# Gate's third and fourth row blocks by seven products instead of eight, and ten early transform steps moved two stages later

## The chip, the cores and the metric

One of the eight cores of a Trainium2 chip runs the kernel. The metric is device microseconds of one execution; the number to predict is the median of three runs. Two names are used throughout: PE is TensorE, the matrix engine, which multiplies a stationary 128x128 block by up to 512 moving columns and adds into a bank of PSUM; DVE (VectorE) and ACT (ScalarE) prepare its operands and take its results out of the banks. POOL (GpSimd) and SP (SyncE) here mostly issue DMAs. Each engine works through its own list of instructions in the order in which they were written.

## What is computed

Two branches over the same input x (2 x 4096 x 640) are mixed by a sigmoid gate:

```python
g = sigmoid((x * gate_w).sum(-1))
a = A(x)      # rfft2 over the 4096 tokens, block-diagonal complex MLP with 4 blocks, soft shrink, irfft2
b = (gelu(x @ w_gate) * (x @ w_up)) @ w_down      # 640 -> 1728 -> 640
out = g * a + (1 - g) * b
```

The change touches the two products `x @ w_gate` and `x @ w_up`, and the first step of the transform in A.

## The kernel before

**The arithmetic.** Everything is fp32 accuracy from fp32r products: an operand is split into a high part (ACT copies it, `high`, L276) and a low part (DVE subtracts the copy, `low`, L279), and a product is three matmuls (high x high, high x low, low x high, `prod`, L472).

**The stages.** First (0 to 1350 us of the span) the products with w_gate and w_up run in three groups of weight tiles: tiles 0 to 3, 4 to 7 and 8 to 13. In each group, all 16 token pairs (512 tokens each, split in two halves of 256) pass by; one token pair with one group is a key, and `keys` (L1311) lists the 48 of them. Then comes the transform with its MLP (to about 1810 us), then the inverse transform with w_down (to the end).

**A quad.** `quad` (L503) does one weight tile (128 gate and 128 up columns) for one token pair. The 640 rows of the weight are five blocks of 128. Blocks 0 and 1 of gate and all of up already go by a seven-product scheme over (gate, up) x (two token halves); blocks 2 and 3 of gate against the first token half are one ordinary product, `g2` by `b21`, of six matmuls into a bank of its own, added on DVE to the partial sum p1:

```python
X = half(); run(X, prod(w["g1"], x_of(o, "b11", ("k4", 0))))
p1 = T("p1"); copy(p1, X)                                        # ACT, L509
C = half(); run(C, prod(w["s3"], x_of(o, "t3", ("k4", 1))))
A = half(); run(A, prod(w["g2"], x_of(o, "b21")))                # six matmuls
nc.vector.tensor_add(p1, A, p1)                                  # L525
run(X, prod(w["s2"], x_of(o, "t2", "t5")), first=False)          # goes on in the bank of p1
```

A quad has 54 matmuls of 256 columns. Bank X is used again and again within it: ACT copies an intermediate sum out (p1, u2, u4), and PE then adds the next product on top. So PE may only go on in a bank when the copy, or the DVE addition, that reads it is over. Three pieces of a quad (`half5`, `half3`, `half4`, L537 to L549) run inside the next quad. Results go to DRAM (`hD`) by a store of 128x4x128 per quad.

**The order around it.** The kernel writes its own schedule. Each quad has seven hooks; `slots` says which small step is issued at which hook of which key. Among them: splitting the next key's tokens (`x_prep`, L426; raw tiles loaded by SP, the sums t1 to t4 formed on DVE, L441), preparing the next group's weights (`w_prep`, L313, eight steps for each weight tile, mostly on DVE), and the first transform steps (`a_split`, `a_gate`, `a_step`, L621 to L634), 64 of them with four matmuls each of 320 columns, placed by `steps_a` (L1382) and `A_POINTS`. The next group's first `w_prep` begins in the last but one key of a group (place 14, hook 10), the others in the last key and the first two of the next group.

**Buffers.** Tiles come from pools of fixed slots: `big` 18, `mid` 14, `small` 18, `tiny` 15, and eight PSUM banks. An instruction that first writes a new tile waits until the last reader of the slot's former tile is done, whichever engine that is, and everything behind it on its own engine waits with it.

Of the kernel before, what the change touches and what calls it, by code (L numbers as in the profile page):

```python
# [15 lines left out]
P = 128  # L16
# [9 lines left out]
NPAIR = 13  # L26

# [186 lines left out]
def spectral_mix_kernel(ctx: ExitStack, tc: tile.TileContext, a):  # L214
# [50 lines left out]
    wdl = dram.tile([P, 7 * 320], F32, name="wdl")  # L265

# [37 lines left out]
    WG, XT, XO, RAW = {}, {}, {}, {}  # L304

# [7 lines left out]
    def w_prep(t, plain=False):  # L313
# [17 lines left out]
        def st0():  # L331
            if not plain:
                gate_high()
            if t < NPAIR:
# [76 lines left out]

    made = lambda key: key[0] == 0 or key == (1, 0)

    def x_raw(key, names=("b11", "b21", "b12", "b22", "k4")):
        d = XT.setdefault(key, {})
        for n in names:
            if key[0] != 1 or made(key) or n != "b12":
                r = d[n] = small([P, 512], name="xraw")
                ld(r, a["xT"][key[1], ("b11", "b21", "b12", "b22", "k4").index(n)])
# [6 lines left out]
    def x_prep(key, k, eng=nc.vector):  # L426
# [43 lines left out]
        return [src, hi, lo]  # L470
# [32 lines left out]
    def quad(key, t, hook):  # L503
# [8 lines left out]

        X = half()
        run(X, prod(w["g1"], x_of(o, "b11", ("k4", 0))))
        p1 = T("p1")
        copy(p1, X)
        hook(0)
# [3 lines left out]
        run(C, prod(w["s3"], x_of(o, "t3", ("k4", 1))))  # L521
        hook(2)
# [5 lines left out]
        u2 = T("u2")  # L528
        copy(u2, X)
        hook(4)  # L530
        old[1]()
        hook(5)
        old[2]()
        hook(6)
        v = {}

        def half5():  # L537
# [3 lines left out]
            gelu(p1, p1)  # L541
            nc.vector.tensor_add(u4, C, u4)  # L542

        def half3():
            run(X, prod(w["s4"], x_of(o, "b22")), first=False)
            h = v["h"] = small([P, 512], name="h")
            gelu(h[:, 256:], X)

        def half4():  # L549
            run(C, prod(w["u2"], x_of(o, "t4")), first=False)  # L550
            nc.vector.tensor_add(u2, C, u2)  # L551
            h = v["h"]
            nc.vector.tensor_mul(h[:, 256:], h[:, 256:], v["u4"])
            nc.vector.tensor_mul(h[:, :256], u2, p1)  # L554
            h_store(key[1], t, h)
        Q.append([half5, half3, half4])

# [753 lines left out]
    keys = [(gr, tp) for gr in range(3) for tp in ([1, 2, 3, 4, 0, *range(5, 16)] if gr == 1 else range(16))]  # L1311
# [59 lines left out]
    A_POINTS = {0: ((1, 3, 4, 5, 8),), 1: ((1, 3, 4, 5, 8), (12, 14, 16, 21, 23)), 2: ((0, 2, 3, 4, 9), (24, 25, 27, 28, 29))}  # L1371
# [10 lines left out]
    steps_a = [(i, j) for i in (*range(2, 12), *range(17, 30), *range(32, 46)) for j in range(1 if i < 16 else 2)]  # L1382
# [18 lines left out]
    for k in range(4):  # L1401
        spread(*((0, 11), (0, 20), (1, 2), (1, 10))[k], w0[k][4 if k else 1:])
    for k, (l, pb) in enumerate(((1, 0), (1, 1), (2, 0), (2, 1))):
# [5 lines left out]
    for gr in range(2):  # L1409
        for k, t in enumerate(groups[gr + 1]):  # L1410
            (i, j), (i2, s) = [((13, 3), (14, 10)), ((14, 3), (15, 8)), ((15, 0), (15, 17)), ((15, 2), (16, 4)), ((15, 3), (16, 12)), ((15, 1), (15, 25))][k]
# [179 lines left out]
```

## Time and profile before

| what | us |
|---|---|
| median of three runs | 2537.26 (2536.99 to 2538.45) |
| the profiled execution, its own time | 2535.42 |
| its span in the trace | 2533.7 |
| PE busy | 2527.2 |
| DVE busy | 2052.9 |
| ACT busy | 1492.7 |

The profiled execution lies 1.84 us under the median, and 1.72 us of its own time are outside the span. PE is busy for all but some 6 us, and the granted clock is full throughout. "Busy" of PE joins overlapping records, so it hides gaps shorter than the overlap; how long a matmul really takes is read from the chain of waits, where a run of matmuls stands with its count and its time.

### The profile page before, as it was taken

To read this page: it belongs to the slowest core of one execution; us is meant where nothing else is said; L and a number is where in the kernel's file an instruction comes from. 1 tells how busy PE (TensorE), PEld (TensorE's weight loads), DVE (VectorE), ACT (ScalarE), POOL (GpSimd) and SP (SyncE) were. 2 spreads that over 40 slices of the span, in tenths; PEclk is the share of its full clock that TensorE was granted. 3 is DMA by queue.
4 is the path that set the end of the run, shared out by engine and by line. 5 is a ranking of instruction groups with operands and counts; after the bars stand their busy time and mean duration, and the time that the engine had idled before them with its cause. 6 is when DMAs were issued, how large, how long until landed. Compare 5 with 4: busy or idle time off the path is not lost.

```text
span 2533.7 us, 54552 instructions
## 1 busy us (share of the span) xinstructions
PE 2527.2 (100%) x20299; PEld 2522.9 (100%) x20299; DVE 2052.9 (81%) x4218; ACT 1492.7 (59%) x3494; POOL 372.4 (15%) x379
## 2 busy tenths in 40 slices
PE   9999999999999999999999999999999999999999
PEld 9999999999999999999999999999999999999999
DVE  7878767777777767766667788888999999899998
ACT  6655555666665655655556788787644444444443
POOL 0000000000000000000003111111133333333332
PEclk9999999999999999999999999999999999999999
DMA  6566647676767677766767354548744444344432
GB/s 231 195 214 197 212 169 234 203 240 210 223 204 253 192 227 226 232 219 209 225 224 229 121 166 141 169 144 263 288 146 150 156 157 139 134 151 157 154 130 103
DMA packets 345982, 483.77 MB, mean 191 GB/s; under 512 B 24748, under 2 KB 221996, under 8 KB 345716
## 3 DMA queue, kind: packets, MB, share of 16 engines
q1 hardware_dynamic: 330884, 438.47, 54.2%
q0 software_dynamic: 14832, 41.82, 4.6%
q8 instruction: 160, 2.62, 0.4%
q14 instruction: 106, 0.87, 0.1%
HBM read 300.55 MB, written 179.64 MB: 190 GB/s over the span
## 4 chain that ended last, share of the span: by engine, by line
PE 96%; DVE 2%; DMA 1%; ACT 1%; issue 0%; SPq 0%; DVEq 0%; ACTq 0%
PE bank L483 54%; PE bank L1234 22%; PE bank L295 14%; PE bank L811 3%; PE bank L645 1%; PE bank L892 1%; PE bank L893 1%; DMA wraw<-in_wgu_dram 0%; DVE w L279 0%; DVE xo L279 0%; PE bank L894 0%; DVE xd L441 0%; DMA xraw<-in_xT_dram 0%; DVE uu L1239 0%; DVE h L554 0%
## 5 line engine op out<-in xcount | busy, mean ns | idle before, releaser
L483 PE MATMUL bank<-xo,w 128*128 128x256 f32 x11676 | 1351.0, 277 | 0.7 <-ACT u L509 0.6
L483 PEld LDWEIGHTS bank<-xo,w 128*128 128x128 f32 x11676 | 1342.2, 188 | 1.7 <-ACT u L509 1.3
L1234 PE MATMUL bank<-wx,ho 128*128 128x320 f32 x3844 | 560.6, 306 | 0.0
L1234 PEld LDWEIGHTS bank<-wx,ho 128*128 128x128 f32 x3844 | 557.1, 188 | 0.0
L509 ACT ACTIVATE u<-bank 128x256 f32<-128x256 f32 x408 | 156.6, 384 | 253.4 <-PE bank L483 248.3
L279 DVE TENSOR_TENSOR ho<-hraw,ho 128x640 fp32r<-128x640 f32 (+3 forms) x384 | 273.8, 754 | 21.4 <-ACT ho L276 18.4
L276 ACT ACTIVATE ho<-hraw 128x640 fp32r<-128x640 f32 x320 | 166.8, 571 | 91.5 <-PE bank L1234 66.0
L509 ACT ACTIVATE p<-bank 128x256 f32<-128x256 f32 x204 | 78.6, 385 | 148.4 <-PE bank L483 61.9
L279 DVE TENSOR_TENSOR xo<-xraw,xo 128x512 fp32r<-128x512 f32 x209 | 143.2, 686 | 23.9 <-ACT xo L276 23.2
L542 DVE TENSOR_TENSOR u<-bank,u 128x256 f32<-128x256 f32 x204 | 85.9, 421 | 89.2 <-ACT u L509 86.6
L279 DVE TENSOR_TENSOR xs<-xr,xs 64x640 fp32r<-64x640 f32 x128 | 104.9, 820 | 58.1 <-ACT xs L276 55.6
L295 PE MATMUL bank<-wm,h 128*128 128x320 f32 (+1 forms) x792 | 137.7, 309 | 0.0
L276 ACT ACTIVATE xo<-xraw 128x512 fp32r<-128x512 f32 x209 | 131.0, 627 | 6.1 <-DMA xraw<-in_xT_dram 4.3
L551 DVE TENSOR_TENSOR u<-bank,u 128x256 f32<-128x256 f32 x204 | 85.5, 419 | 60.0 <-PE bank L483 59.3
L647 DVE TENSOR_TENSOR as<-bank,as 64x320 f32<-64x320 f32 x256 | 113.7, 483 | 24.9 <-ACT as L646 23.7
L295 PEld LDWEIGHTS bank<-wm,h 128*128 128x128 f32 (+1 forms) x792 | 117.9, 185 | 1.4
L598 POOL MEMSET h<- 64x512 f32 x16 | 8.4, 522 | 749.8 <-PE bank L645 437.5
L483 PE MATMUL bank<-wx,ho 128*128 128x320 f32 x764 | 116.3, 307 | 0.0
L525 DVE TENSOR_TENSOR p<-bank,p 128x256 f32<-128x256 f32 x204 | 86.6, 424 | 36.5 <-PE bank L483 31.9
L483 PEld LDWEIGHTS bank<-wx,ho 128*128 128x128 f32 x764 | 112.1, 188 | 0.0
L276 ACT ACTIVATE ho<-hs 128x640 fp32r<-128x640 f32 (+1 forms) x128 | 69.0, 570 | 70.2 <-DVE ho L279 51.1
L646 ACT ACTIVATE as<-bank 64x320 f32<-64x320 f32 x256 | 96.8, 427 | 16.4 <-PE bank L645 13.9
(168 smaller groups left out, 3669.6 us busy)
## 6 DMA issues: line engine op xcount, KB each, us to landing
xo<-xD SPq DMA_DIRECT2D x124, 512.0 KB
xraw<-in_xT_dram SPq DMA_DIRECT2D x225, 256.0 KB
hD<-h SPq DMA_DIRECT2D x224, 256.0 KB
hraw<-hD SPq DMA_DIRECT2D x128, 320.0 KB
xD<-xo POOLq DMA_DIRECT2D x64, 512.0 KB, 4.3
sc<-scr SPq DMA_DIRECT2D x65, 320.0 KB
xr<-in_x_dram SPq DMA_DIRECT2D x64, 320.0 KB
scr<-as SPq DMA_DIRECT2D x64, 320.0 KB
```

Source lines behind the costliest of these rows:

```text
L276: nc.scalar.activation(dst, src, AF.Copy, scale=scale)
L279: eng.tensor_sub(dst, src, hi.bitcast(F32))
L295: nc.tensor.matmul(dst, l, r, start=i == 0, stop=i == len(ops) - 1)
L483: nc.tensor.matmul(dst, l, r, start=first and i == 0, stop=i == len(ops) - 1, skip_group_check=True)
L509: copy = lambda d, s_: nc.scalar.activation(d, s_, AF.Copy)
L525: nc.vector.tensor_add(p1, A, p1)
L542: nc.vector.tensor_add(u4, C, u4)
L551: nc.vector.tensor_add(u2, C, u2)
L646: nc.scalar.activation(stg[hi, cs], pa[lo, :320], AF.Copy)
L647: nc.vector.tensor_add(stg[hi, cs], pa[hi, :320], stg[hi, cs])
L811: nc.tensor.matmul(pz[:, kp * P:(kp + 1) * P], SC[b, c, kp][:, o:o + P], ft, start=True, stop=True)
L1234: nc.tensor.matmul((X, Y)[k], *op, start=n[k] == 0 and not (more and k), stop=n[k] == tot[k] - 1, skip_group_check=True)
```

## The change

For token pairs 3 to 14 of groups 0 and 1 (`deep`), the product of gate's blocks 2 and 3 leaves the quads. Two weight tiles (t, t+1) x two row blocks form a 2x2 matrix of weight blocks, two row blocks x the first halves of two token pairs (tp, tp+1, tp odd) a 2x2 matrix of token blocks, and their product is made by seven block products of three matmuls each (`deep_parts`) instead of eight. The seven run one at a time between the pieces of the two quads that follow, in two banks, and each is added on DVE to one of four waiting partial sums:

```diff
+    def deep(key):
+        return key[0] < 2 and FIRST <= key[1] < 15
...
+        def go(m, n, first, dst):
+            if n not in b:
+                b[n] = bank()
+            acc = b[n][:, :256]
+            for i, (l, r) in enumerate(prod([wa[m]], [xa[m]])):
+                nc.tensor.matmul(acc, l, r, start=first and i == 0, stop=i == 2, skip_group_check=True)
+            nc.vector.tensor_add(dst, acc, dst)
+        def f0():
+            go("m2", 0, True, p11)
+        def f1():
+            go("m1", 1, True, p11)
+            g11()
...
+        E.extend([(0, f0), (1, f1), (2, f2), (3, f3), (0, f4), (1, f5), (3, f6), (0, f7)])
```

In such a quad the ordinary product is skipped, and gelu and the last multiplication (`end`) wait until the seven products are in:

```diff
-        A = half()
-        run(A, prod(w["g2"], x_of(o, "b21")))
-        nc.vector.tensor_add(p1, A, p1)
+        if not dp:
+            A = half()
+            run(A, prod(w["g2"], x_of(o, "b21")))
+            nc.vector.tensor_add(p1, A, p1)
```

The weight sums for it are made by `w_deep` (four small DVE operations, then a split), the token sums by `x_deep` (two DVE operations of 256 columns at each of two places, five splits, two of them of 512 and three of 256 columns). Group 0 stores the split token sums to a new DRAM tensor `xA` through POOL (`mid` tiles of 128x1024 and `small` tiles of 128x512), group 1 loads them back through SP and no longer loads and splits `b21`. Half of the result stores become two of 128x2x128.

The schedule changes with it: no transform step is left in group 0, and ten keys of group 2 have three instead of two; group 1 begins with token pairs 1, 2, 0; the first weight tile of the next group is prepared from the start of a group's last key on, not from the key ahead:

```diff
-    keys = [... ([1, 2, 3, 4, 0, *range(5, 16)] if gr == 1 else range(16))]
+    keys = [... ([1, 2, 0, *range(3, 16)] if gr == 1 else range(16))]
-    steps_a = [(i, j) for i in (*range(2, 12), *range(17, 30), *range(32, 46)) for j in range(1 if i < 16 else 2)]
+    steps_a = [(i, j) for i in (*range(17, 30), *range(32, 46)) for j in ((0, 1) if i < 32 else (0, 1, 2) if 32 < i < 43 else (0, 2))]
-            (i, j), (i2, s) = [((13, 3), (14, 10)), ((14, 3), (15, 8)), ...
+            (i, j), (i2, s) = [((14, 1), (15, 0)), ((14, 3), (15, 8)), ...
```

The order on the engines, first on PE inside a deep stretch of group 0. Before, a quad of token pair 4 and a transform step in it (w_152 to w_156 are blocks of weights; rows of one line stand together with their count):

```order
L483 MATMUL bank<-xo,w_152 128x256 x9
L483 MATMUL bank<-xo,w_418 128x256 x9
L483 MATMUL bank<-xo,w_358 128x256 x9
L483 MATMUL bank<-xo,w_152 128x256 x6
L483 MATMUL bank<-xo,w_358 128x256 x9
L483 MATMUL bank<-xo,w_780 128x256 x3
L483 MATMUL bank<-xo,w_781 128x256 x3
L645 MATMUL bank<-xs,f_828 128x320 x2
L483 MATMUL bank<-xo,w_418 128x256 x6
```

Now, a quad with four of the seven products (L693) in it:

```order
L562 MATMUL bank<-xo,w_298 128x256 x9
L693 MATMUL bank<-xo,w_158 128x256 x3
L562 MATMUL bank<-xo,w_286 128x256 x9
L562 MATMUL bank<-xo,w_654 128x256 x9
L693 MATMUL bank<-xo,w_158 128x256 x3
L562 MATMUL bank<-xo,w_654 128x256 x9
L693 MATMUL bank<-xs,w_1014 128x256 x3
L562 MATMUL bank<-xo,w_540 128x256 x3
L562 MATMUL bank<-xo,w_541 128x256 x3
L562 MATMUL bank<-xo,w_286 128x256 x6
L693 MATMUL bank<-xo,w_1014 128x256 x3
```

The six matmuls in the middle are gone, products of three stand between the others, and the transform step's matmuls (L645) are no longer in this group.

Second, DVE at the end of group 0, where the next group's first weight tile begins to be prepared (in brackets what an instruction waits for; wt are weight sums, p1, u2, u4, h and pb partial sums, xo split tokens). Before:

```order
L542 TENSOR_TENSOR u4_5388<-bank_5317,u4_5388 128x256 [waits Activation_49]
L525 TENSOR_TENSOR p1_5376<-bank_5404,p1_5376 128x256 [waits PE_49]
L339 TENSOR_TENSOR wt_5414<-wraw_5285 128x256 [waits DMAHW0_49]
L340 TENSOR_TENSOR wt_5416<-wt_5414,wraw_5283 128x256 [waits DMAHW7_49,DVE_49]
L279 TENSOR_TENSOR xo_5402<-xraw_5281,xo_5402 128x512 [waits DMAHW6_49,DMASW2_49,Activation_49]
L441 TENSOR_TENSOR xd_5420<-xraw_5279,xraw_5277 128x512 [waits DMAHW5_49,DMAHW4_49,DMAHW1_49]
L345 TENSOR_TENSOR wt_5416<-wraw_5283,wraw_5285 128x256
```

Now:

```order
L346 TENSOR_TENSOR wt_5406<-wraw_5187 128x256 [waits DMAHW2_49,DVE_49]
L347 TENSOR_TENSOR wt_5408<-wt_5406,wraw_5185 128x256 [waits DMASW2_49,DMAHW1_49,DVE_49,PE_49]
L640 TENSOR_TENSOR u4_5422<-bank_5315,u4_5422 128x256 [waits DMAHW0_49,Activation_49]
L352 TENSOR_TENSOR wt_5408<-wraw_5185,wraw_5187 128x256
L353 TENSOR_TENSOR wt_5406<-wraw_5185,wt_5408 128x256 [waits DVE_49]
L281 TENSOR_TENSOR xo_5411<-xd_5355,xo_5411 128x512 [waits DMASW6_49]
L694 TENSOR_TENSOR pb_4880<-bank_5439,pb_4880 128x256
L281 TENSOR_TENSOR w0_5404<-wraw_5185,w0_5404 128x5x128
L616 TENSOR_TENSOR p1_5396<-bank_5446,p1_5396 128x256
L365 TENSOR_TENSOR wt_5407<-wraw_5187,wraw_5185 128x128
L366 TENSOR_SCALAR wt_5407<-wraw_5187 128x128
L694 TENSOR_TENSOR p1_5296<-bank_5399,p1_5296 128x256
```

The second weight sum (wt, L340 before, L347 now) waited for its loads and for DVE itself; now it also waits for PE, and between the steps of the weights stand the additions of the seven products (L694).

Third, PE at that same place. Before (the quad's six matmuls of `g2` by `b21` fill bank 5404, which the addition L525 above reads):

```order
L483 MATMUL bank_5392<-xo_5092,w2_510 128x256 x6
L483 MATMUL bank_5392<-xo_5060,w2_510 128x256 x3
L483 MATMUL bank_5404<-xo_5131,w0_277 128x256 x6
L483 MATMUL bank_5366<-xo_5156,w2_510 128x256 x6
L483 MATMUL bank_5366<-xo_463,w2_510 128x256 x3
L483 MATMUL bank_5288<-xo_5259,w3_407 128x256 x3
L483 MATMUL bank_5288<-xo_5259,w3_408 128x256 x3
L483 MATMUL bank_5317<-xo_5300,w1_153 128x256 x6
```

Now:

```order
L562 MATMUL bank_5386<-xo_5242,w2_364 128x256 x6
L562 MATMUL bank_5386<-xo_469,w2_364 128x256 x3
L693 MATMUL bank_5399<-xs_5082,w4_1132 128x256 x3
L562 MATMUL bank_5286<-xo_5006,w3_786 128x256 x3
L562 MATMUL bank_5286<-xo_5006,w3_787 128x256 x3
L562 MATMUL bank_5315<-xo_5041,w1_424 128x256 x6
L693 MATMUL bank_5439<-xo_5117,w4_1132 128x256 x3
L562 MATMUL bank_5515<-xo_5102,w0_283 128x256 x6
L562 MATMUL bank_5515<-xo_5144,w0_283 128x256 x3
L693 MATMUL bank_5399<-xs_5146,w0_392 128x256 x3
```

The wait for PE of L347 is one for the third row, the product that reads xs_5082, a `small` tile of the same pool as wt. Behind it, PE goes on in the banks 5315, 5439 and 5399, each read by DVE between (L640, L694, L694).

## Rows read from the trace of the kernel before

**Rows 1.** The profile's page: the span, and busy time of each engine.
```profile
span 2533.7 us, 54552 instructions
PE 2527.2 (100%) x20299; PEld 2522.9 (100%) x20299; DVE 2052.9 (81%) x4218; ACT 1492.7 (59%) x3494; POOL 372.4 (15%) x379
```

**Rows 2.** The chain of work that ended last: start us, us, what, with its count.
```profile
192.34 21.56 PE bank L483 x190
...
437.38 0.29 PE bank L645 x2
...
764.86 56.58 PE bank L483 x499
```

**Rows 3.** Busy us and count of each engine, granted clock, DMA share, by stretches of groups 0, 1, 2.
```profile
core 0: us, PE busy (x) PEld busy (x) DVE busy (x) ACT busy (x) POOL busy (x), PEclk, DMA share, GB/s
41.65:292.76 251.11, 250.63 (x2193) 250.32 (x2193) 199.19 (x435) 151.21 (x360) 21.80 (x41) 1.00 0.62 207
...
519.00:776.00 257.00, 257.00 (x2237) 257.00 (x2236) 186.85 (x415) 155.94 (x366) 0.00 (x0) 1.00 0.70 218
...
827.00:1180.00 353.00, 353.00 (x3085) 353.00 (x3084) 249.30 (x567) 206.97 (x497) 6.57 (x13) 1.00 0.70 220
```

**Rows 4.** Instructions on PE in order of time, end of group 0.
```profile
373.77 3.45 PE L483 MATMUL bank<-xo,w 128*128 128x256 f32 x29
377.37 4.81 PE L483 MATMUL bank<-xo,w 128*128 128x256 f32 x38 [0.15 <-ACT u L509]
```

**Rows 5.** Instructions on DVE in order of time, end of group 0: start, duration, idle before.
```profile
367.74 0.43 DVE L525 TENSOR_TENSOR p<-bank,p 128x256 f32<-128x256 f32 x1 [0.86 <-PE bank L483]
...
368.87 0.68 DVE L279 TENSOR_TENSOR xo<-xraw,xo 128x512 fp32r<-128x512 f32 x1
369.47 0.68 DVE L441 TENSOR_TENSOR xd<-xraw 128x512 f32<-128x512 f32 x1
370.07 0.41 DVE L345 TENSOR_TENSOR wt<-wraw 128x256 f32<-128x256 f32 x1
370.41 0.42 DVE L346 TENSOR_TENSOR wt<-wraw,wt 128x256 f32<-128x256 f32 x1
370.75 0.82 DVE L279 TENSOR_TENSOR w<-wraw,w 128x640 fp32r<-128x640 f32 x1
371.48 0.41 DVE L551 TENSOR_TENSOR u<-bank,u 128x256 f32<-128x256 f32 x1
...
372.48 0.28 DVE L358 TENSOR_TENSOR wt<-wraw 128x128 f32<-128x128 f32 x1
372.69 0.22 DVE L359 TENSOR_SCALAR wt<-wraw 128x128 f32<-128x128 f32 x1
372.82 0.68 DVE L279 TENSOR_TENSOR xo<-xd,xo 128x512 fp32r<-128x512 f32 x1
```

**Rows 6.** The chain of work that ended last, end of group 0.
```profile
375.61 0.70 DVE xd L441
...
376.34 0.55 ACT xo L276
...
376.94 0.39 ACT u L509
```

**Rows 7.** Busy us of the engines in the stretch where group 1 ends (columns of rows 3).
```profile
806.00:812.00 6.00, 6.00 (x56) 6.00 (x55) 5.97 (x19) 4.45 (x12) 0.00 (x0) 1.00 0.76 212
812.00:818.00 6.00, 6.00 (x56) 6.00 (x55) 5.60 (x18) 4.17 (x14) 0.00 (x0) 1.00 0.90 293
```

**Rows 8.** Groups of DVE instructions, 41.65 to 292.76 us: count, busy, mean ns, idle before.
```profile
L647 DVE TENSOR_TENSOR as<-bank,as 64x320 f32<-64x320 f32 x38 | 16.9, 482 | 0.3
L525 DVE TENSOR_TENSOR p<-bank,p 128x256 f32<-128x256 f32 x40 | 16.8, 421 | 8.1 <-PE bank L483 7.7
...
L279 DVE TENSOR_TENSOR xs<-xr,xs 64x640 fp32r<-64x640 f32 x20 | 16.4, 820 | 5.4 <-ACT xs L276 5.1
...
L632 DVE SCALAR_TENSOR_TENSOR xr<-xr,gw 128x640 f32<-128x640 f32 x10 | 8.3, 826 | 0.3
```

**Rows 9.** Groups of ACT instructions in the same stretch.
```profile
L509 ACT ACTIVATE u<-bank 128x256 f32<-128x256 f32 x81 | 31.0, 383 | 47.8 <-PE bank L483 47.0 <-issue 0.3
...
L276 ACT ACTIVATE xo<-xd 128x512 fp32r<-128x512 f32 x40 | 25.0, 626 | 10.6 <-DVE xd L441 10.6
...
L509 ACT ACTIVATE p<-bank 128x256 f32<-128x256 f32 x41 | 15.8, 385 | 27.0 <-PE bank L483 17.1 <-ACT xo L276 9.9
```

**Rows 10.** The page's DMA issues: count, KB each, median us to landing.
```profile
xD<-xo POOLq DMA_DIRECT2D x64, 512.0 KB, 4.3
```

More of the change, by code (lines that the diff above doesn't have):

```diff
@@ L265, in spectral_mix_kernel @@
     wdl = dram.tile([P, 7 * 320], F32, name="wdl")
+    xA = {t: dram.tile([P, 3584], F32, name=f"xA_{t}") for t in range(FIRST, 15, 2)}
     fny = consts.tile([P, 8], F32, name="fny")
@@ L416, in x_raw @@
         for n in names:
-            if key[0] != 1 or made(key) or n != "b12":
+            if (key[0] != 1 or made(key) or n != "b12") and not (key[0] == 1 and deep(key) and n == "b21"):
                 r = d[n] = small([P, 512], name="xraw")
@@ L511, in quad @@
         old = Q.pop() if Q else [lambda: None] * 3
+        dp = deep(key)
+        ahead_ = dp and key[1] % 2 == 1
         X = half()
         run(X, prod(w["g1"], x_of(o, "b11", ("k4", 0))))
-        p1 = T("p1")
+        if ahead_:
+            if t % 2 == 0:
+                PB[t] = big([P, 5, 256], name="pb")
+            p1, u2 = (PB[t - t % 2][:, 2 * (t % 2) + k] for k in range(2))
+        elif dp and t % 2 == 0:
+            p1 = PB[t][:, 4]
+        else:
+            p1 = T("p1")
         copy(p1, X)
+        extra(0)
         hook(0)
@@ L533, in quad @@
         old[2]()
+        extra(3)
         hook(6)
@@ new lines, in end, with extra @@
+        def end():
+            nc.vector.tensor_mul(u2, u2, p1)
+            if ahead_:
+                half_store(key[1], t, 0, u2)
+            else:
+                h_store(key[1], t, v["h"])
+        if dp:
+            PEND[key[1], t] = p1, lambda: gelu(p1, p1), end
+        Q.append([half5, half3, half4])
+        if dp and not ahead_ and t % 2:
+            deep_parts(key[0], key[1] - 1, t - 1)
+    PB, E = {}, []
+    def extra(k):
+        while E and E[0][0] == k:
+            E.pop(0)[1]()
@@ L1402, in spectral_mix_kernel @@
         spread(*((0, 11), (0, 20), (1, 2), (1, 10))[k], w0[k][4 if k else 1:])
+    for t, i, s in ((0, 2, 1), (2, 2, 11), (4, 15, 25), (6, 16, 13)):
+        for k, f in enumerate(w_deep(t)):
+            spread(i, s + 2 * k, [f])
+    for i, (gr, tp) in enumerate(keys):
+        if deep((gr, tp)) and tp % 2:
+            p, f = x_deep(gr, tp)
+            if gr == 0:
+                spread(i, 22, p[:1])
+                spread(i, 24, p[1:])
+            for k, q in enumerate((0, 3, 1, 4, 2)):
+                if gr:
+                    spread(i, 20 + 3 * k, f[q])
+                else:
+                    spread(i + 1, 1 + 3 * k, f[q][:1])
+                    spread(i + 1, 2 + 3 * k, f[q][1:])
     for k, (l, pb) in enumerate(((1, 0), (1, 1), (2, 0), (2, 1))):
```

123 lines of the change are left out of this document (111 added, 12 removed).

## Prediction

> **What bounds the kernel now.** I read the page first: PE is busy for 2527.2 of 2533.7 us, and no other engine comes near [rows 1]. Such a figure can hide short stalls, so the second view is the chain of waits, where long runs of matmuls of the quads stand with their counts: 190 in 21.56 us and 499 in 56.58 us, 113.4 ns each, and two of the transform's 320 columns in 0.29 us, 145 ns each [rows 2]. The third view splits the span by stage: in groups 0, 1 and 2, PE is busy to within 0.5 us at a granted clock of 1.00, which is the 2.4 GHz level, while DVE has 79, 73 and 71% and ACT about 60% [rows 3]. So in the stages that change, time is the number of matmuls times 113.4 ns, plus waits, and there are hardly any waits. The one to look at is the end of group 0: 29 matmuls begin at 373.77 and the next ones at 377.37, 3.60 us where 29 x 113.4 ns make 3.29, so 0.31 us are lost [rows 4]. There DVE works through one unbroken list from 367.74 on, with weight sums (wt), token sums (xd) and partial sums mixed [rows 5]; ACT waits for a token sum, then makes its split, and only then the copy that PE waits for [rows 6]. DVE is at 5.97 of 6 us where group 1 ends as well, without a loss yet [rows 7]. At the group ends nothing is spare on DVE.
>
> **The change part by part: the matmuls.** 12 token pairs x 4 tiles x 2 groups are 96 quads with six matmuls less each, 576. They come back as 24 groups of seven products of three, 504. So 72 fewer, x 113.4 ns = -8.16 us. A product of three matmuls between longer ones costs no more per matmul by rows 2, whose 190 hold runs of three (s4's) as well. The moved transform steps keep their matmuls: ten steps x 4 x 145 ns leave group 0 and return in group 2, zero.
>
> The Trainium skill ("TensorE: Matmul & The Clock Gate", section "Wait — 56ns, not 53.3ns?") gives a warm matmul as columns over 2.4 GHz plus about 2.5 ns. Its estimate is 109.2 ns for 256 columns and -7.86 us for the 72. The rows show 113.4, so the measurement decides.
>
> **What is added on other engines in the middle of the stages.** A group of four quads has seven additions where it had four of 0.42 us [rows 8]. In group 0, a pair of keys thus gets six more additions, four token sums of 256 columns and 768 more columns to split, about 5.4 us of DVE. It loses two transform steps. One step has four additions at 0.48, two low parts at 0.82 and one gate product at 0.83 [rows 8], 4.4 us. So DVE gets lighter in group 0 and some 2% heavier in group 1, where loaded `b21` splits fall away. Group 2 gets ten steps in ten keys of 35.3 us: 71% + 4.4/35.3 = 83%. Group 0 ran at 79% without a wait worth naming [rows 3], so I put 0 here, at most 0.5. ACT keeps four-tenths free. The stores and the new loads ride on DMA queues at a share of 0.62 to 0.70 [rows 3]. Group 1 reads 1.28 MB more in a pair of keys of 51 us, 25 GB/s on 218. By the order, each new load can be issued at least 166 matmuls (19 us) ahead of its use; one old load of 512 KB at the end of group 1 keeps 91 (10.3 us) where the shortest had 112. A store of that size lands in 4.3 us [rows 10], so nothing.
>
> **Group 0's end, the weak place.** DVE is one list. In the changed order the second weight sum of the next group (L347, in `w_prep`) reuses a `small` slot that PE reads until the product with xs_5082 is over. DVE stands still until then, and everything behind it is late: u4_5422, for which PE waits six matmuls (0.68 us) later; pb_4880, 12 matmuls (1.36 us) later; p1_5296, 24 matmuls (2.72 us) later. The weight steps that were spread from the last key but one now begin here. From that wait to u4_5772, DVE's list holds 42 operations of 256 columns, 7 of 512, 3 of 640 and 14 of 128 (3 of them by a scalar). Starts in an unbroken list stand 0.33 to 0.34, 0.60, 0.73, 0.21 and 0.13 us apart [rows 5], so 42 x 0.335 + 7 x 0.60 + 3 x 0.73 + 11 x 0.21 + 3 x 0.13 = 23.2 us. PE has 180 matmuls in that stretch, 20.4 us. So PE loses 2.8 us, and 0.2 for the hand-overs at both ends. ACT's queue behind the token sums adds about what it cost before [rows 4, 6], 0.3 to 0.4. In all 3.4 us.
>
> Just ahead of it ACT has a stop of the same kind: the split of a token sum into a `mid` slot that PE still reads, with the copy of bank X behind it. 0.63 + 0.39 us [rows 9] and a hand-over of 0.1 stand against six matmuls of 0.68: 0.4 us.
>
> **Group 1's end.** The same wait on an xs tile, and the same list but one operation of 512 shorter: 22.6 against 20.4 us, 2.2 + 0.2 + 0.4 = 2.8 us.
>
> Both are bounded below by nothing lost (DVE takes up what PE does not need yet) and above by the list at full durations, below. The 0.31 us lost before [rows 4] goes; it lies in the same place and is in the 3.4.
>
> **Sum.** -8.16 + 0.4 + 3.4 + 2.8 - 0.3 = -1.9 us. The profiled execution would come to 2533.5, and the median, 1.84 us above it, to 2535.4.
>
> **The rivals.** First, that group ends hide themselves: if PE meets the late results only where it has other banks to go on with, what remains is the matmuls alone, -8.2 - 0.3, so 2528.8. For it: the list at the end of group 0 is unbroken before as well and cost only 0.31 us [rows 4, 5]. Against it: waits on a bank are in PE's order, and 23.2 us do not fit into 20.4. It decides if DVE's list is under 21 us. Chance 0.17; up to 2532 it counts as faster by more than 0.2%.
>
> Second, slower: the bank X comes round sooner. With the six matmuls gone, PE goes on in X 18 matmuls (2.04 us) after the product that ACT copies, where it had 24 (2.7 us). ACT needs 0.39 us for the copy, and 0.63 for each token split ahead of it [rows 9], so two splits ahead still fit (1.65 us) and a third (2.28 us) costs 0.24 us. In group 0, ACT was ahead of PE for these copies, with 17.1 and 47.0 us of waiting for PE [rows 9]. That speaks against it. If half of the 96 quads lost 0.24, that is 11.5 us, and the time 2547; it is slower by more than 0.2% from 30 such losses on. Chance 0.08.
>
> Third, DVE instructions take their full durations one after the other: 0.42, 0.69, 0.82, 0.28 and 0.22 us [rows 5] for the list make 28.6 us against 20.4 at either end, so 8 us twice, and 2545.3. The rows speak against it: 370.07, 370.41 and 370.75 are starts of operations that last 0.41 and 0.42. Chance 0.02.
>
> The Trainium skill has this third case as a rule ("VectorE: DVE Perf Modes", section "Terms", DRAIN): the pipeline is flushed after each operation, and the next cannot issue until it is empty. What the rows show is starts 0.08 us ahead of the recorded end, so the flush, if the record holds it, is not paid in a list.
>
> **How the numbers follow.** About 0.2%, 5.1 us, is what a measurement of this kernel can tell from no change. The forecast, losses at both group ends that eat most of the gain, has 0.73 and its own range is 2533 to 2538: the losses from 4.5 (no ACT share, shorter list) to 9 us (list broken by waits on ACT too). Faster has the first rival and a tail, 0.18; slower the second and third, 0.10; same 0.72. The range of 8 in 10 takes in half of the first rival's and the losses' upper bound, from 2530.0 to 2539.5.
>
> **What would show it.** PE's count is down by 72 at 113.4 ns. At the ends of groups 0 and 1, PE rows with idle time released by DVE additions (L640, L694) or ACT copies (L588) sum to about 4 and 3 us; DVE is at 100% there for some 20 us, and L347 waits for PE. In the middle of groups 0 and 1, a pair of keys takes 6 x 113.4 ns less and has no idle time. Group 2's keys with three steps take 0.58 us more and nothing else. Wrong would be a wait that comes back at each key of a deep stretch, or group ends without PE idle time.

## The result, and the profile after

The changed kernel takes 2546.9 us (median of nine, 2543.8 to 2559.5); the kernel before, timed beside it, 2537.0. The ratio is 1.005, 95% interval 1.0033 to 1.0066: slower by about half a per cent, outside the predicted range of 2530.0 to 2539.5. Two of the nine executions (2558.4 and 2559.5) lie some 12 us above the median of the other seven, 2546.6; such executions, at least 6 us above the slowest of the others of their kernel, are called late, and what they are is told under "late executions" below.

The profile's page of the changed kernel shows the 72 matmuls gone and the span longer all the same (before: [rows 1]):

```profile
span 2544.6 us, 54675 instructions
PE 2528.4 (99%) x20227; PEld 2519.7 (99%) x20227; DVE 2086.1 (82%) x4340; ACT 1491.2 (59%) x3504; POOL 387.4 (15%) x409
```

Where the time went is read by counting matmuls in equal stretches. First three stretches of the kernel before, then the same of the changed one (group 0 with its end, group 1 with its end, group 2):

```profile
core 0: us, PE busy (x) PEld busy (x) DVE busy (x) ACT busy (x) POOL busy (x), PEclk, DMA share, GB/s
30.00:425.00 395.00, 394.37 (x3457) 393.73 (x3456) 306.90 (x695) 230.43 (x561) 31.91 (x60) 1.00 0.63 207
425.00:829.00 404.00, 403.89 (x3515) 403.66 (x3514) 300.12 (x681) 248.53 (x590) 3.68 (x7) 1.00 0.70 220
829.00:1390.00 561.00, 560.95 (x4901) 560.69 (x4901) 392.31 (x896) 326.70 (x794) 34.12 (x52) 1.00 0.71 222
```

```profile
30.00:425.00 395.00, 391.85 (x3428) 390.53 (x3427) 301.02 (x718) 208.56 (x528) 48.02 (x90) 1.00 0.65 221
425.00:829.00 404.00, 397.20 (x3402) 393.82 (x3402) 298.71 (x691) 235.99 (x564) 2.66 (x5) 1.00 0.72 236
829.00:1390.00 561.00, 560.83 (x4882) 560.64 (x4881) 425.75 (x968) 355.29 (x850) 32.44 (x48) 1.00 0.73 231
```

At the rate of before (404 / 3515 = 0.1149 us a matmul) the 3402 matmuls of the second stretch would have taken 391.0 us, so 13.0 us are lost there. In the first stretch it is 395 - 3428 x 0.1143 = 3.3 us, plus 1.3 because 40 transform matmuls of 145 ns instead of 113.4 are no longer among them: 4.6. In the third it is 2.2 - 1.3 = 0.9. Together 18.5 us lost against 8.2 saved: +10.3, of the span's +10.9. Most of the loss sits in group 1 and its end, and the waits of PE say for what:

```profile
PE bank L562 <- ACT pb L588: 4.7, 5, 1.0
PE bank L562 <- ACT p L588: 3.1, 2, 1.7
```

The columns are total us, times, longest. The second row belongs to the ends of groups 0 and 1; the rows left out are of 0.7 us and less in all, at the group ends or outside these stages, but for one of 1.2 us in a later stage that the kernel before has too. The first row is new: five equal stops in group 1, one in each pair of token pairs with seven products except the first (3 and 4). This is one of them, in order of time (start, duration, idle time before and its releaser):

```profile
541.64 3.22 PE L562 MATMUL bank<-xo,w 128*128 128x256 f32 x27
...
542.34 0.73 ACT L278 ACTIVATE xs<-xr 64x640 fp32r<-64x640 f32 x1
543.10 0.82 DVE L281 TENSOR_TENSOR xs<-xr,xs 64x640 fp32r<-64x640 f32 x1 [0.47 <-ACT xs L278]
543.95 0.42 DVE L650 TENSOR_TENSOR pb<-bank,pb 128x256 f32<-128x256 f32 x1
544.29 0.42 DVE L651 TENSOR_TENSOR h<-h,u 128x256 f32<-128x256 f32 x1
544.62 0.42 DVE L694 TENSOR_TENSOR pb<-bank,pb 128x256 f32<-128x256 f32 x1
...
545.07 0.42 ACT L589 ACTIVATE pb<-pb 128x256 f32<-128x256 f32 x1 [2.01 <-DVE pb L694]
545.39 0.36 ACT L588 ACTIVATE pb<-bank 128x256 f32<-128x256 f32 x1
...
545.81 4.06 PE L562 MATMUL bank<-xo,w 128*128 128x256 f32 x30 [0.95 <-ACT pb L588]
549.71 0.46 PE L818 MATMUL bank<-xs,f 128*128 128x320 f32 x2
```

Read it backwards. PE waits for ACT's copy of bank X (545.39). ACT had been idle for 2.01 us, but with a gelu (L589) at the head of its list, and the copy behind it. The gelu needs the seventh product's sum, DVE's L694 at 544.62. DVE has that sum fourth in its list, behind the low half of a transform split (L281, 543.10), and the split waits 0.47 us for its high half, which ACT made at 542.34. So the wait runs ACT, DVE, ACT, PE, in three lists that are each kept in order. The 27 matmuls from 541.64 need 27 x 113.4 ns = 3.06 us, so PE is ready at 544.70 and goes on at 545.81: 1.11 us, five times 5.5. The stop costs more than itself: the 30 matmuls behind it take 549.71 - 545.81 = 3.90 us, where 30 x 113.4 ns make 3.40. That is 0.50 us again, behind each of the five, 2.5 in all; it lies in gaps of some 0.1 us each, too short for this view to name what ended them.

### The profile page after: what moved, and what is told of

Read it like the earlier page. It is cut to its first block, busy times and chain, and to the rows that moved or that the text cites. A ratio compares the mean times of both kernels' runs of the same rounds, so it can differ in the third digit from the quotient of the medians.

```text
span 2544.6 us, 54675 instructions
## 1 busy us (share of the span) xinstructions
PE 2528.4 (99%) x20227; PEld 2519.7 (99%) x20227; DVE 2086.1 (82%) x4340; ACT 1491.2 (59%) x3504; POOL 387.4 (15%) x409
## 4 chain that ended last, share of the span: by engine, by line
PE 95%; DVE 2%; ACT 1%; issue 1%; DMA 0%; SPq 0%; ACTq 0%; DVEq 0%
PE bank L562 51%; PE bank L1407 22%; PE bank L297 14%; PE bank L984 3%; PE bank L693 2%; PE bank L818 1%; PE bank L1066 1%; PE bank L1065 1%; DVE w L281 0%; PE bank L745 0%; PE bank L1067 0%; DMA rl<-in_w2l_dram 0%; DVE xs L281 0%; DVE xo L281 0%; DMA scr<-is 0%
## 5 line engine op out<-in xcount | busy, mean ns | idle before, releaser
L562 PE MATMUL bank<-xo,w 128*128 128x256 f32 x11100 | 1319.9, 278 | 9.2 <-ACT pb L588 4.7
L562 PEld LDWEIGHTS bank<-xo,w 128*128 128x128 f32 x11100 | 1293.8, 188 | 13.0 <-ACT pb L588 5.7
L281 DVE TENSOR_TENSOR ho<-hraw,ho 128x640 fp32r<-128x640 f32 (+3 forms) x384 | 273.8, 755 | 20.1 <-ACT ho L278 17.1
L588 ACT ACTIVATE u<-bank 128x256 f32<-128x256 f32 x312 | 119.1, 382 | 134.3 <-PE bank L562 126.0
L281 DVE TENSOR_TENSOR xs<-xr,xs 64x640 fp32r<-64x640 f32 x128 | 104.9, 820 | 77.4 <-ACT xs L278 75.8
L640 DVE TENSOR_TENSOR u<-bank,u 128x256 f32<-128x256 f32 x204 | 85.8, 421 | 88.1 <-ACT u L588 87.3
L281 DVE TENSOR_TENSOR xo<-xraw,xo 128x512 fp32r<-128x512 f32 x191 | 131.0, 686 | 23.3 <-ACT xo L278 21.9
L820 DVE TENSOR_TENSOR as<-bank,as 64x320 f32<-64x320 f32 x256 | 113.7, 483 | 30.0 <-ACT as L819 28.6
L278 ACT ACTIVATE xo<-xraw 128x512 fp32r<-128x512 f32 x191 | 119.7, 627 | 5.7 <-DMA xraw<-in_xT_dram 4.4
L278 ACT ACTIVATE xs<-xr 64x640 fp32r<-64x640 f32 x128 | 94.0, 734 | 20.4 <-DMA xr<-in_x_dram 18.5
L588 ACT ACTIVATE p<-bank 128x256 f32<-128x256 f32 x132 | 50.5, 382 | 94.5 <-DVE h L651 51.5
L1330 POOL TENSOR_TENSOR hraw<-hs,hraw 128x640 f32<-128x640 f32 (+1 forms) x62 | 80.1, 1311 | 121.3 <-DVE ho L281 121.3
```

What stands on the lines that cost most here:

```text
L278: nc.scalar.activation(dst, src, AF.Copy, scale=scale)
L281: eng.tensor_sub(dst, src, hi.bitcast(F32))
L562: nc.tensor.matmul(dst, l, r, start=first and i == 0, stop=i == len(ops) - 1, skip_group_check=True)
L588: copy = lambda d, s_: nc.scalar.activation(d, s_, AF.Copy)
L820: nc.vector.tensor_add(stg[hi, cs], pa[hi, :320], stg[hi, cs])
L1330: eng.tensor_add(d["a11"][k], d["s2"][k], d["a11"][k])
```

## Experiments on the five stops

Each run is told against the kernel before, timed beside it, median 2536.3 to 2537.5 us in every set.

**The split moved** by two points, behind the copy, in the odd keys of group 1:

```diff
+        if 16 < i < 32 and keys[i][1] > 4 and j and keys[i][1] % 2:
+            sp = (14, 16, 18, 21, 23)
```

The points were (12, 14, 16, 21, 23): both halves of the split and the gate product move, and so do the points that are counted back from the first, such as that of their load.

> The changed kernel, with one number changed: in the odd keys of group 1 from 5 on, the second transform step's split starts at point 14 instead of 12, behind the copy of bank X that PE waits for, its second half at 16, the gate product at 18. The gelu stays where it is. Theory A (round trip through the split): DVE no longer stands behind ACT's high half of the split when the seventh product is to be added, so the gelu and the copy come in time; the five stops of 0.95 us go or fall under 0.3 us each, 2540 to 2543. Theory B (bank X comes round too soon for the gelu and the copy, whatever DVE does): the stops stay, 2546 to 2548.

Measured: 2541.1 us, four of twelve executions late (2551.9 to 2555.8); span 2537.9 against 2544.6. The row of five is gone from group 1; what PE still waits for between 425 and 788 us is this:

```profile
PE bank L818 <- DMA f<-in_f_dram: 0.5, 1, 0.5
PE bank L562 <- ACT p L588: 0.4, 1, 0.4
PE bank L693 <- DVE pb L694: 0.4, 1, 0.4
```

Theory A's number holds: 5.8 us from three points of a table, with all products, splits and copies in place. Theory B is out, since the window of 18 matmuls on bank X is the same and the copies now come in time.

**Only DVE's half of the split moved**, ACT's left where it was:

```diff
         high(xs[hi], t[hi])
-        low(xs[lo], t[hi], xs[hi])
+        f = lambda: low(xs[lo], t[hi], xs[hi])
...
+            back(i, 14, lambda d=d: d.pop()())
```

`high` (ACT) stays at point 12; `f`, the low half (DVE), is put off to point 14.

> The changed kernel; in the odd keys of group 1 from 5 on ACT's high half of the second step's first split stays at point 12, and only DVE's low half is issued later, at point 14 (behind the gelu and the copy of bank X in the program). Theory A (the stop comes from DVE, which stands 0.47 us for ACT's high half and then takes 0.8 us for the low one, ahead of the sum that the gelu needs): the sum is 1.2 us earlier and the five stops go, 2540 to 2542. Rival D (ACT's own 0.73 us for the high half, ahead of gelu and copy in its queue, is what makes the copy late): the stops stay, 2546 to 2548.

Measured: 2545.3 us. At the same place (start, duration, idle before):

```profile
544.72 0.42 ACT L589 ACTIVATE pb<-pb 128x256 f32<-128x256 f32 x1 [0.59 <-DVE pb L694]
545.04 0.37 ACT L588 ACTIVATE pb<-bank 128x256 f32<-128x256 f32 x1
...
545.63 1.67 DVE L281 TENSOR_TENSOR xs<-xr,xs 64x640 fp32r<-64x640 f32 x2
...
547.33 0.42 DVE L640 TENSOR_TENSOR u<-bank,u 128x256 f32<-128x256 f32 x1
...
547.81 1.99 PE L562 MATMUL bank<-xo,w 128*128 128x256 f32 x15 [0.20 <-DVE u L640]
```

ACT now waits 0.59 us for the sum instead of 2.01, although its own 0.73 us for the high half stand where they stood: rival D is out as the cause of the stop of 0.95. But two low halves now stand in a row on DVE (1.67 us), ahead of u's addition (L640), and PE stops five times for that, 0.2 us each as this view counts them. The time missed A's 2540 to 2542 by 3 us and is only 0.7 us below the rival's: of the 5.8 us that moving the whole split gave, 1.6 arrived. Moving work a little further down DVE's list is not the same as taking it out of the busy place.

**Only the gelu moved**, behind the copy:

```diff
             go("m3", 1, False, p12)
-            g12()
             e22()
 
         def f7():
+            g12()
             e12()
```

> The changed kernel, with one line moved: the gelu of the pair's third left half (g12) is issued with the last token sum's multiplication, in the next quad behind the copy of bank X, and not right behind the seventh product. Theory A (round trip): in group 1 the trace of the changed kernel has five stops of PE of about 0.95 us at L562, all for ACT's copy of bank X, where ACT stood 2.0 us in front of this gelu, which waits for DVE's sum, which stands in DVE's list behind the low half of a transform split that waits for ACT. With the gelu behind the copy the row 'PE bank L562 <- ACT pb L588' (4.7 us, 5 times) should be gone, and with it 5 to 7 us: 2540 to 2542. Theory B (bank X comes round too soon, 18 matmuls, and ACT is late with whatever it has queued): the copy is late as before, the five stops stay within 1 us of their sum, 2546 to 2548.

Measured: 2544.7 us, two of seven executions late, so Theory A's 2540 to 2542 was missed. Its wait did go from the copy pb (L588), and came back one copy later:

```profile
543.19 0.42 ACT L589 ACTIVATE pb<-pb 128x256 f32<-128x256 f32 x1 [1.74 <-DVE pb L694]
543.64 0.73 ACT L278 ACTIVATE xs<-xr 64x640 fp32r<-64x640 f32 x1
...
544.39 0.38 ACT L588 ACTIVATE u<-bank 128x256 f32<-128x256 f32 x1
...
544.83 2.89 PE L562 MATMUL bank<-xo,w 128*128 128x256 f32 x21 [0.84 <-ACT u L588]
```

ACT still stands 1.74 us in front of the gelu, and now it is the copy u, behind the gelu and the next high half, that is late by 0.84 us. Theory A in the form "the gelu must not stand ahead of that copy" fell with this; what holds is that any ACT work which waits for that late sum makes the next copy late. The cause is the lateness of the sum, which the split's place sets.

**The transform steps put back** into group 0, as before the change:

```diff
-    steps_a = [(i, j) for i in (*range(17, 30), *range(32, 46)) for j in (... (0, 1, 2) ...)]
+    steps_a = [(i, j) for i in (*range(2, 12), *range(17, 30), *range(32, 46)) for j in range(1 if i < 16 else 2)]
```

The table of points for group 2 goes back to two steps with it.

> The changed kernel with the transform steps where the kernel before had them: ten in the keys of group 0 (points 1, 3, 4, 5, 8), none added in group 2. Theory A: group 1 and the group ends are as in the changed kernel, its five stops stay; in group 0 the steps at the start of a key are far from the seventh product in quad 1 and cost at most 1 us: 2546 to 2548. Rival E (any transform step beside a deep pair costs): ten more stops of 0.3 us and up, 2550 or more. In the run of the move alone 3 of 12 executions were some 11 us above the others, in the kernel before none of 30: if the move brings them, none of them appears here.

Measured: 2551.5 us, five executions within 3.5 us. Waits of PE from 60 to 360 us (group 0), then from 425 to 800 us (group 1):

```profile
PE bank L562 <- ACT pb L588: 0.9, 3, 0.3
PE bank L562 <- ACT h L589: 0.7, 4, 0.2
```

```profile
PE bank L562 <- ACT pb L588: 4.8, 5, 1.0
```

The five stops of group 1 stay, as A said. In group 0, where the changed kernel has no step and no such waits, seven appear, smaller than E's 0.3 and up (0.2 to 0.3 us); there the steps lie at the start of a key. The time is E's: a transform step beside a pair with seven products costs in either group, and taking the steps out of group 0 was worth about 4.5 us to the changed kernel. The seven waits make only 1.6 us of that; stretches at the slow pace told below stand in group 0's trace as well, and no run took the rest apart. No execution of the five is late.

## Experiments on the parts

**The move alone**, on the kernel before (its two tables of points and steps taken from the changed kernel, nothing else):

> The kernel before, with nothing of the products: only the table of transform steps is that of the changed kernel, so that group 0 has no transform step and ten keys of group 2 have three. Theory A: the move by itself costs nothing, as the prediction had it: 2536 to 2538.5. Theory C: the move costs, in group 2 or because the first half of the transform is finished later: 2539 or more. It leaves nothing of the computation out.

Measured: 2538.4 us, ratio 1.0014 (1.0002 to 1.0026). Nine of the twelve executions lie from 2535.5 to 2539.3, as the kernel before does; three lie at 2546.7 to 2550.6. So the move costs nothing but these three, which the kernel before has in none of 30 beside it.

**Seven products in group 0 alone**:

```diff
-        return key[0] < 2 and FIRST <= key[1] < 15
+        return key[0] < 1 and FIRST <= key[1] < 15
```

The weight sums of group 1 (`w_deep`) go with it.

> The changed kernel, with the seven products in group 0 alone; group 1 computes the unchained product as before. Theory A: 36 matmuls of 113.4 ns saved (4.1 us), the stop ahead of group 0's end and the group's end stay (4.05 us by the trace of the changed kernel), group 1 has none of its five stops and no longer end: 2536 to 2538.5. Theory B (the splits in the middle of the stage lose time wherever the products are): half of the changed kernel's loss stays, 2540 to 2543.

Measured: 2537.05 us (ratio 1.0009, 0.9997 to 1.0021), three of twelve executions late (2547.6 to 2549.3): as A had it. Group 0 gives its 4.1 us and loses about as much at its end; by these medians the whole 10 us are group 1's.

**The last pair of keys as before**, with the split moved:

```diff
-        return key[0] < 2 and FIRST <= key[1] < 15
+        return key[0] < 2 and FIRST <= key[1] < 13
-            ... [((14, 1), (15, 0)), ...
+            ... [((13, 3), (14, 10)), ...
```

> The changed kernel with the split moved as in the run that gave 2541.1, and with the last pair of keys of groups 0 and 1 (13, 14) computed as before, the first weight preparation back at its earlier place (13, 3), (14, 10). 12 matmuls come back, 1.36 us. Theory of the prediction (the ends of groups 0 and 1 lose about 7 us because the weight steps of the next group meet the deep pair's DVE work there): the stops at both ends go, all but the 0.3 us that the kernel before had, 2535 to 2537. Rival (the longer list of weight steps, or the missing transform steps' place, makes the loss whether the last pair is deep or not): 2539.5 or more.

Measured: 2535.7 us, one of twelve executions late (2544.5, the profiled one), against 2541.1 with the last pair in: the theory's number. From 360 to 425 us, where the changed kernel had four rows with 2.6 us, one is left, the one that the kernel before had:

```profile
PE bank L562 <- ACT u L588: 0.2, 1, 0.2
```

From 788 to 829 us PE waits for nothing. 12 matmuls were given back (1.4 us) and 5.4 us net gained by the two medians; without late executions, each against the kernel before beside it, it is 3.6. That fits the prediction's account, weight steps that meet the last deep pair. But the run also puts the first weight preparation back to its earlier key, and no run does one of the two alone, so which of them freed the ends is not shown.

**Both edits**, the split moved and the gelu behind the copy:

> The changed kernel with both earlier edits: the second step's split in the odd keys of group 1 at points 14, 16, 18, and the gelu g12 behind the copy of bank X. The first edit alone gave 2541.1, the second alone shortened the longest stop at each group's end from 1.6 to 1.8 us to some 0.7 in the trace. Theory A: the two act in different places and add up, 2538.5 to 2540. Rival: with the split moved, the gelu is no longer what the copy waits for at the group ends either, and nothing more is gained: 2540.5 to 2542.

Measured: 2541.7 us, but of ten executions four are late (2550.1 to 2555.4); the other six lie at 2537.9 to 2542.3, where the split alone had eight at 2538.8 to 2541.5 beside its four late ones. So the rival held: the gelu's place adds nothing once the split is out of the way. In its trace PE's waits for ACT's copy p at the group ends fell from 3.1 to 0.5 us, but in group 1 (425 to 800 us) PE waits 1.4 us for that copy and 1.4 us for DVE's L694, where it was 0.4 and 0.4 with the split alone: the gain of the ends is given back.

## Experiments on the late executions

The profiled execution with both edits was a late one. Its chain of work that ended last, and that of the changed kernel's profiled execution (not late), for the same kind of run in group 0 (start, us, count):

```profile
99.96 18.37 PE bank L562 x156
```

```profile
99.92 15.87 PE bank L562 x140
```

18.37 / 156 = 117.8 ns, 15.87 / 140 = 113.4 ns: the same matmul, no wait in either, granted clock 1.00 in both. A window of the late one, then of the changed kernel:

```profile
60.00:100.00 40.00, 40.00 (x342) 40.00 (x341) 26.11 (x60) 18.70 (x46) 3.20 (x6) 1.00 0.53 181
```

```profile
60.00:100.00 40.00, 40.00 (x356) 40.00 (x355) 27.42 (x63) 19.45 (x48) 3.72 (x7) 1.00 0.52 182
```

14 matmuls fewer in 40 us; from 280 to 320 us it is 342 against 356 again. By the starts of its matmuls the slow pace holds from 30 to 377 us: 347 us x 4.4 / 117.8 = 13 us, about what the late executions are late. The one other late execution with a trace, that of the kernel with the last pair as before, shows the same, there from 29 to 327 us (11 us):

```profile
60.00:100.00 40.00, 40.00 (x342) 40.00 (x342) 25.86 (x60) 18.63 (x46) 3.20 (x6) 1.00 0.52 186
```

In both it ends at a stop (PE rows of the first):

```profile
375.05 1.22 PE L562 MATMUL bank<-xo,w 128*128 128x256 f32 x9
376.11 0.52 PE L693 MATMUL bank<-xs,w 128*128 128x256 f32 x3
376.91 2.33 PE L562 MATMUL bank<-xo,w 128*128 128x256 f32 x18 [0.29 <-ACT h L588]
...
379.41 2.54 PE L562 MATMUL bank<-xo,w 128*128 128x256 f32 x21
381.79 0.50 PE L693 MATMUL bank<-xs,w 128*128 128x256 f32 x3
```

Before the 0.29 us stop nine matmuls take 376.11 - 375.05 = 1.06 us, 117.8 ns each; after it 21 take 381.79 - 379.41 = 2.38, 113.3 each. The slow pace is also in the changed kernel's profiled execution, for 39 us at the start of group 1, where the kernel before ran fast:

```profile
392.94 39.22 PE bank L562 x333
```

```profile
392.95 44.43 PE bank L483 x392
```

117.8 against 113.3 ns: 1.5 us there. But the slow pace is not the change's own. The kernel before has it too, in another place, between 506 and 533 us; this is the longest of its rows there, 117.8 ns a matmul:

```profile
518.91 11.43 PE bank L483 x97
```

**One transform step back in key 2**, on the kernel with both edits (`steps_a` begins with `(2, 0)`, one step less in group 2):

> The kernel with both edits (split at points 14, 16, 18 in the odd keys of group 1; gelu behind the copy) and with one transform step back in key 2 of group 0, the only one there; nine instead of ten are added in group 2. In that kernel 4 of 10 executions lay 8 to 15 us above the others, and the profiled one was such a one: from 60 us on until the next stop, some 325 us later, PE held 342 matmuls in 40 us where a fast execution held 355. Theory P (pace): PE comes out of the start at one of two paces, 113.3 or 117.8 ns a matmul, and keeps it while matmuls of 256 columns follow each other without a break; the 320-column matmuls of a transform step and its short break set it back. Then one step in key 2 is enough, and no execution of about 10 lies more than 5 us above the fastest; median 2538.5 to 2540. Rival Q (the late executions have another cause, such as the heavier group 2 or a transfer): 3 to 5 of 10 are late as before.

Measured: 2537.5 us, two of twelve late (2548.0, 2551.0), the others 2535.5 to 2540.3. Theory P's "no late one" fell, and so did Q's "three to five". The profiled execution is not one of the late two, so what happened in those is not known.

**The same step on the kernel with the last pair as before**:

> The kernel with the last pair of keys computed as before and the split moved (2535.7 in its run, one of twelve executions late), and with one transform step back in key 2 of group 0. Theory P: no late execution, all within 5 us, median 2534.5 to 2536. Rival Q: one late execution or more of about 12.

Measured: 2534.6 us against 2536.6 for the kernel before, ratio 0.9991 (0.9982 to 0.9999), none of eleven late (2530.9 to 2537.0). The one version here whose interval lies below the kernel before, only just, by 2 us.

**Group 0 alone, last pair as before, one step in key 2**:

> Seven products in group 0 alone, last pair of keys as before, weight preparation at its earlier place, one transform step back in key 2. Saved: 5 pairs x 6 matmuls = 30, 3.4 us. By the traces group 0's stops are then those of the kernel before and group 1 is untouched, so 3 us should be left as gain: 2533 to 2534.5, and no late execution. Rival: something else in group 0 takes the gain (small stops at each pair, as they were seen in group 1): 2535.5 to 2537.5.

Measured: 2533.25 us, ratio 0.9995 (0.9984 to 1.0006), two of twelve late (2546.2, 2546.4), the others 2532.4 to 2536.4. The gain of 3 us is there; "no late execution" was wrong again.

**A matmul cut in two**, on the kernel with both edits and no step in group 0:

```diff
+            if cut and i == 2:
+                for c in (slice(0, 128), slice(128, 256)):
+                    nc.tensor.matmul(dst[:, c], l, r[:, c], start=False, stop=False, skip_group_check=True)
```

`cut` is set in the first quad of keys 3 to 15 of group 0 and of three keys of group 1.

> The kernel with both edits (split later, gelu behind the copy), of which 4 of 10 executions were late, with no transform step in group 0. In the first quad of keys 3 to 15 of group 0 and of the first three keys of group 1 one matmul of 256 columns is issued as two of 128; nothing else is changed. Theory P2 (PE has two paces for a row of equal matmuls, 113.3 and 117.8 ns, keeps the one it has, and a matmul of another width can bring it from the slow to the fast one, as the transform's do): the stretch from 400 to 440 us, which held 340 to 345 matmuls in 40 us in every kernel with the move so far, holds 350 or more, and no execution of about 10 is more than 5 us above the fastest; the cuts themselves cost at most 16 x 0.1 us; median 2537 to 2540. Rival (what ends the slow pace is PE standing still, not a matmul of another width): the stretch stays below 346, and 3 to 5 of 10 are late by 8 us and more.

Measured: 2539.3 us, eleven executions from 2538.1 to 2541.5, none late, where the same kernel without cuts had four of ten. One window:

```profile
400.00:440.00 40.00, 40.00 (x352) 39.98 (x351) 31.42 (x82) 24.25 (x64) 0.53 (x1) 1.00 0.70 222
```

The count of 352 between 400 and 440 us is as P2 said but proves little: the kernel with the split moved alone held 354 there without any cut, so the expectation's "in every kernel with the move" was wrong. The missing late executions speak for P2, but not strongly. Over all kernels without a step in group 0 and without cuts, 19 of 79 executions were late, and at that rate eleven without a late one come by chance about once in twenty; the kernel with the last pair as before and one step had none of eleven as well, without any cut. The trace says more. Behind the end of group 0, 46 matmuls from 395.17 to 400.59 us start 117.8 ns apart; gaps of 0.04 and 0.10 us follow, and the seven matmuls ahead of the first cut one, at 402.36, are 118 ns apart again. Behind the cut the row is fast:

```profile
402.70 24.43 PE bank L566 x215
```

That is 113.6 ns each. In six other traces the slow row at this place lasted until a transform step at 431 to 438 us. So a cut did end the slow pace here, seen once. That the cuts in group 0 are what kept the late executions away is argued from this, not shown.

## Why the prediction was wrong, step by step

**What bounds the kernel** held: PE throughout, with a granted clock of 1.00. "Matmuls times 113.4 ns, plus waits" is not the whole of it: in the prediction's own trace 216 matmuls between 506 and 533 us ran at 117.8, 1.0 us that is no wait.

**The 72 matmuls, -8.16 us**: right. The page counts 20227 instead of 20299, and rows of them run at 113.4 ns as in [rows 2], except where the slow pace holds.

**The ends of groups 0 and 1, 0.4 + 3.4 + 2.8 us**: right in place and in the sum, but the sum owes something to luck. At group 0's end, PE and DVE in order of time:

```profile
375.64 0.84 PE L562 MATMUL bank<-xo,w 128*128 128x256 f32 x6
375.84 0.43 DVE L347 TENSOR_TENSOR wt<-wt,wraw 128x256 f32<-128x256 f32 x1 [2.05 <-PE bank L693]
...
376.65 0.96 PE L562 MATMUL bank<-xo,w 128*128 128x256 f32 x6 [0.17 <-DVE u L640]
378.26 0.63 PE L693 MATMUL bank<-xo,w 128*128 128x256 f32 x3 [0.64 <-DVE pb L694]
...
386.46 4.05 PE L562 MATMUL bank<-xo,w 128*128 128x256 f32 x33
390.73 0.42 ACT L589 ACTIVATE pb<-pb 128x256 f32<-128x256 f32 x1 [1.76 <-DVE pb L694]
...
391.97 2.27 PE L562 MATMUL bank<-xo,w 128*128 128x256 f32 x17 [1.47 <-ACT p L588]
```

L347 waits 2.05 us for PE's product with the xs tile; then PE stops for u and for pb, DVE's additions, as the prediction had it, and for p. Start to start, less 113.4 ns a matmul, the stops are 0.33, 0.93, 0.25 (ahead of 379.99) and 1.77 us, 3.3 in all against 3.4; the one ahead of them (364.64, where 364.17 was due) is 0.47 against 0.4. At group 1's end the same four are 0.33, 0.33, 0.25 and 1.98, 2.9 against 2.8. But the longest of them, 1.77 and 1.98, is not a late addition that PE meets in a bank. It is ACT's copy p, and ACT had stood 1.76 us in front of a gelu ahead of it: the same coupling as in the five stops. DVE's long list did make the gelu's operand late, as the prediction had it; that the delay reaches PE by way of ACT it did not have. With the gelu behind the copy, PE goes on there at 390.69, 0.21 us late by starts, and some smaller stops follow.

**The middle of the stages, "I put 0 here, at most 0.5"**: this is the step that failed, by about 10 us, all of it in group 1 (13.0 less 2.9). The five stops make 5.5 by start to start, and the matmuls right behind them 2.5 more. The slow pace takes about 1.4 us more in this stretch than in the kernel before (216 matmuls between 450 and 477 us and some 150 from 805 to 825 are the most of it, against 216 of the kernel before). The last 0.7 is left in gaps of 0.1 to 0.3 us, which no run took apart. Moving the split gave 5.8 of median, not all of the 8.0, since smaller stops stand in its trace instead (0.4 to 0.5 us each, in the rows above). That it all hangs on group 1's products is seen from the counts: with products in group 0 alone and the last pair as before, the stretch from 425 to 829 us holds 3512 matmuls, as good as the 3515 of before, and with the split moved 3457. The slow pace around group 1's start, 1.5 us, lies mostly ahead of 425 us, in the 4.6 us of the first stretch: 0.5 + 3.3 for the end, 1.2 for the pace, less the 0.3 of before. The reason given for the zero was a share: DVE some 2% heavier in group 1 and still under the 79% at which group 0 had run without waits, ACT four-tenths free. A share says nothing about a wait that goes through two engines. ACT was idle for 2.01 us at the very moment when its copy was late, and DVE for 0.47.

**The second rival** had the right place (the copy of bank X, 18 matmuls after the product) and, at 2547, even the time, but not the cause; that its time came out is luck. It asked how many of ACT's 0.63 us splits fit ahead of the copy. What stood ahead was a gelu whose operand comes from DVE, put there by the change itself (f6: product, sum, gelu, all at one point), and a transform split shared by ACT and DVE in the same quad. Each new operation was costed by its duration; none was followed to who makes its operand and what stands ahead of that one in its list.

**The third rival** has a slip, 0.69 for the 0.68 us of [rows 5]; its 28.6 us are worked out with 0.68.

**The move of the transform steps, 0**: right for the bulk of executions, but it had a price that the prediction did not look for: group 0 without a step runs at the slow pace in some executions. Three of twelve were late with the move alone, none of 30 without; for the changed kernel two of nine. Over all runs it is 19 of 79 with no step in group 0, 4 of 35 with one, and none of 109 with all ten, 104 of them the kernel before.

**What would show it**: "wrong would be a wait that comes back at each key of a deep stretch" is what came, at every second key from token pair 5 on.

## What to carry to other kernels

When a change adds an operation on engine A that needs a result of engine B, write down what stands ahead of that result in B's list, and whether any of it waits for A: if it does, what stands behind the new operation can be late, however idle both engines look in the shares. Then move the shared work (here a split) out of that place, or the new operation a round trip away from it. Where the last unit of a stage meets the first preparations of the next, try it without the extra work in that unit: here 12 matmuls given back, with the first preparation moved ahead again, bought some 4 to 5 us.

## What the runs showed of the hardware

A row of equal 256-column matmuls without waits ran at one of two paces, 113.4 or 117.8 ns each, at the same granted clock of 1.00, and kept to it for up to 347 us. Both paces stand in the trace of the kernel before as well, where nothing was changed. Stops of PE changed the pace in both directions: one of 0.29 us ended the slow one, one of 1.47 us at group 0's end was followed by 333 matmuls at the slow one. In the traces kept here, every slow row of more than 100 matmuls in the three groups ended at a stop of PE, at a pair of the transform's 320-column matmuls, or, once, at a matmul cut in two. Not every such pair ended one: in the changed kernel the first pair behind those 333 did not, and the second, 3.4 us later, did. What makes the pace, and which one follows a break, is not settled; one step early in group 0 still left two late executions of twelve. With one matmul cut in two in most keys of group 0 none of eleven was late, so in this kernel, at least, something uneven among long, even rows of matmuls may make the time steadier.

A stop of PE cost more than its own length: behind each of five stops of 1.11 us, the next 30 matmuls took 0.50 us more than 30 x 113.4 ns.
